# An order table that starts from the key weights, in a one-core adaLN mixer

## The chip, the cores and the metric

The kernel runs on one core of a Trainium2 chip. A core has a matrix engine (TensorE, PE, with a weight load queue PEld beside it), a vector engine (VectorE, DVE), a scalar engine (ScalarE, ACT), a general engine (GpSimd, POOL) and a sync engine (SyncE, SP) that issues transfers. Each engine works through its own list of instructions in order; engines wait for one another through semaphores. Data lie in on-chip memory of 128 partitions; matmul results go to eight banks of PSUM. The metric is device time of one launch in microseconds (us).

## The reference, cut to what matters

One sequence x of 2048 rows of 448, a conditioning row c, bfloat16 throughout:

```python
mod = (silu(c) @ w_mod).reshape(1, 6, 1, 448)      # sa, ca, ga, sb, cb, gb
h = layernorm(x) * (1 + ca) + sa
x = x + ga * A(h, wqkv, w_phi, wo)
h = layernorm(x) * (1 + cb) + sb
x = x + gb * B(h, w_in, w_sp, b_sp, w_out)

def A(h):            # 16 heads of 28
    q, k, v = h @ wqkv, by head
    phi(t) = [softmax(t @ w_phi), softmax(-t @ w_phi)]        # 56 features
    o = phi(q) @ (phi(k)^T v) / (phi(q) . sum(phi(k)) + 1e-6)
    return o @ wo

def B(h):
    z1, z2 = split(gelu(h @ w_in))                  # 896 each
    g = w_sp @ layernorm(z2) + b_sp                 # w_sp is 2048 x 2048, over the rows
    return (z1 * g) @ w_out
```

## The kernel before, in words

The rows are taken as 16 tiles of 128. The whole computation of the fast path is a set of small step functions (`fast_path`, from L538), and a written table, `ORDER` (L482), says in which order they are issued. A word of the table is step:arguments@PSUM bank/engine; the engine is V for DVE, S for ACT, G for POOL and Y for SP, and a step without one has a fixed engine. The loop at L1245 to L1257 walks the table once, under a manual schedule, so the instructions of each engine stand in the order in which the table names their steps, and an engine that waits for one step holds all later ones. Nothing else sets the order. The words, by stage:

- **Loads.** `ld:...` issues one transfer (L664 to L682). wq, wk, wv are the 448x448 parts of wqkv, x0 to x5 the rows of x in groups of 1, 1, 2, 4, 4 and 4 tiles, phi is w_phi, wsa, wca, wsb, wcb are the shift and scale parts of w_mod, wmga and wmgb its two gates, wo, win0, win1, wout the remaining weights, bsp the bias of the row mixing. `W:t,u` (L1076) loads a piece of w_sp with a transposing transfer. The transfers of SP and ACT use eight semaphores in turn.
- **Front.** `du:n` are n matmuls on zeros (L734). `ct` and `ce` make silu(c). Wq and Wk are multiplied by w_phi beforehand ("folded"): `FTq`, `FTk` transpose the raw weights on PE (L824), `ETq`, `ETk` copy the transposes out of PSUM (L828 or L830), `PFq`, `PFk` multiply by a block-diagonal w_phi (L840), `EPq`, `EPk` copy the folded blocks out (L828, L830). `csA`, `ccA` (L769) turn shift and scale into columns, `esA` and `ecA` copy them; `SHk`, `SHq`, `SHv` (L783) make the shift's row of each weight and `SCk`, `SCq`, `SCv` (L801, L803) scale its rows. `csB`, `ccB`, `esB`, `ecB`, `SHw`, `SCw` do the same for w_in, and `YB`, `YE` for its first half.
- **First layer norm.** `l1s` statistics on DVE, `l1e`, `l1r`, `l1a` the factors and the normalised rows; `X` and `XE` transpose tiles 0 to 3 on PE, `T1` the others by transposing transfers on SP.
- **Attention sums.** Per tile: `kM` (L881), `kE`, `kF` two exponentials on ACT (L884), `kS` their row sums on DVE (L895), `kR` reciprocals (L899), `kP` the products (L902, DVE or POOL), `vM` and `vC` (L889, L892), and `kA` (L912), which adds the tile to one accumulator in PSUM. After the last `kA`, `KV` copies the accumulator out (L918, L920). `gr:0`, `gr:1` (L940) and `ge` spread the two gates over the rows; `wos`, `wts` (L946) multiply them into wo and w_out.
- **Attention output.** `qM` (L929), `qE`, `qF` (L934) for the queries; per tile `nM` (L957), `nX`, `nC`, `nS`, `nV`, `nT` (L976, the product of numerator and reciprocal), `nA` (L982), a transposing transfer `T2` (L863), and `wM` or `wN` (L992; `wN` adds x by one more matmul, L990), `wR` (L997, L999), `wQ` sums of squares.
- **Second layer norm and w_in.** `lA` to `lD`, `l2r`, `l2a`, the transfer `T3`, then `zM` and `zG` (z2, L1038), `zQ`, `zA` to `zD`, `zW`, `zN` its layer norm, `yM` and `yG` (z1, L1068, L1071).
- **Row mixing and output.** `gM` (L1084) multiplies w_sp by the last column block directly; the first six column blocks go by seven products instead of eight for a 2x2 split: `tT`, `sS` form differences and sums of the operands, `pM` (L1148) the products, `pc`, `pb` (L1171, L1172, POOL), `uA`, `uB`, `uW`, `cA` (L1175, DVE) combine them and `cX` (L1200) multiplies by z1. `oM` (L1097) is the product with w_out, `oE` adds x, `oD` writes a tile of 112 KB out; the last tile is done in two halves by `oH`, `oG` (L1106) and `oF` (L1110).

`guard`, `guard2`, `guard3` and `read` decide whether the sums were in a safe range; a general path stands behind them and is not run on these inputs.

Of the kernel before, what the change touches and what calls it, by code (L numbers as in the profile page):

```python
# [1305 lines left out]
```

## Time and profile before

| | us |
|---|---|
| median of 3 runs | 250.22 (249.93 to 250.77) |
| the profiled execution's own time | 250.54 |
| its span | 248.7 |
| PE busy | 239.2 (96%) |
| DVE busy | 187.5 (75%) |
| ACT busy | 115.7 (47%) |
| POOL busy | 128.3 (52%) |
| chain that ended last | PE 81%, DVE 10%, ACT 4%, DMA 2% |

The span runs from the first instruction to the last; the execution's own time holds also what lies around it, 1.8 us here. A row of the timeline gives start, length, engine, line, operation, output and input, and in square brackets the idle time before it with what ended it. A row with "x12" joins twelve instructions that follow one another. The chain of waits follows the end of the span back from each step to what released it. Matmuls overlap at their ends, so the length of a group of them is somewhat more than the distance to the next.

### The profile page before, as it was taken

Reading aid. Unit: us, or ns where it says so; the run is one execution under the profiler, and the core shown is the slowest. Engines: PE = TensorE matmul, PEld = TensorE weight load, DVE = VectorE, ACT = ScalarE, POOL = GpSimd, SP = SyncE. Lnnn points to the kernel's source line nnn. Section 1 sums busy time; section 2 is a strip of 40 time slices with the busy share of each in tenths; the row PEclk is TensorE's granted clock in tenths of the full one; section 3 lists DMA queues with packets and bytes.
Section 4 is the critical chain, followed back from the end, with each engine's and each line's share of the span. In section 5 each row is a group of like instructions: output and inputs, shape, how many; then the busy total and the mean of one; then the engine's idle time right before and its main releaser. Section 6 shows DMA issues by size and latency. Waiting matters only on the chain.

```text
span 248.7 us, 4220 instructions
## 1 busy us (share of the span) xinstructions
PE 239.2 (96%) x1520; PEld 127.2 (51%) x1528; DVE 187.5 (75%) x374; ACT 115.7 (47%) x231; POOL 128.3 (52%) x172
## 2 busy tenths in 40 slices
PE   8899999999889999999999999999999999999992
PEld 6755566566535555544444444444444544444652
DVE  2889998977988988967357985858899754727652
ACT  3999887738889888787878110000010000000000
POOL 4768878576678556747855449601541901401000
PEclk9999999999999999999999999999999999999998
DMA  7998989970595634782100960009930120000022
GB/s 190 307 279 166 206 171 234 204 191 0 100 167 115 128 88 86 168 154 60 42 0 4 152 102 0 3 0 155 187 79 3 55 74 0 3 0 3 18 78 86
DMA packets 68800, 25.23 MB, mean 101 GB/s; under 512 B 58401, under 2 KB 68642, under 8 KB 68770
## 3 DMA queue, kind: packets, MB, share of 16 engines
q1 hardware_dynamic: 68160, 24.41, 48.9%
q10 hardware_dynamic: 610, 0.46, 0.6%
q8 instruction: 14, 0.23, 0.4%
q14 instruction: 16, 0.13, 0.2%
HBM read 8.87 MB, written 1.84 MB: 43 GB/s over the span
## 4 chain that ended last, share of the span: by engine, by line
PE 81%; DVE 10%; ACT 4%; DMA 2%; issue 1%; DVEq 0%; ACTq 0%; SPq 0%
PE f_psum L1148 29%; PE f_psum L1068 10%; PE f_psum L1038 9%; PE f_psum L1097 8%; PE f_psum L1084 6%; PE f_psum L992 4%; PE f_psum L929 3%; PE f_psum L881 3%; DVE f_ksum L895 2%; PE f_psum L889 2%; DVE f_t L976 2%; DMA f_oo<-f_oo 2%; PE f_psum L734 2%; DVE f_phik L902 1%; PE f_psum L957 1%; PE f_psum L783 1%
## 5 line engine op out<-in xcount | busy, mean ns | idle before, releaser
L1148 PEld LDWEIGHTS <-f_z2n 128*128 128x128 bf16 x192 | 18.7, 98 | 22.4
L1148 PE MATMUL f_psum<-f_wsp,f_z2n 128*128 128x512 bf16 x119 | 27.1, 379 | 0.1
L1068 PE MATMUL f_psum<-f_hT,f_win 112*128 112x512 bf16 x112 | 26.3, 379 | 0.0
L1038 PE MATMUL f_psum<-f_win,f_hT 112*128 112x448 bf16 (+1 forms) x128 | 26.1, 352 | 0.0
L1148 PE MATMUL f_psum<-f_hT,f_Eq 128*128 128x512 bf16 x92 | 22.3, 379 | 0.2
L1168 ACT COPY f_Eq<-f_psum 128x512 f32<-128x512 f32 x4 | 2.3, 586 | 40.0 <-PE f_psum L1148 40.0
L1097 PE MATMUL f_psum<-f_wout,f_z1T 128*128 128x448 bf16 x105 | 20.4, 352 | 0.0
L1071 ACT ACTIVATE f_z1T<-f_psum,f_yb 128x512 bf16<-128x512 f32 x28 | 17.8, 686 | 3.3 <-PE f_psum L1068 3.3
L934 ACT ACTIVATE f_Eq<-f_psum 112x1024 bf16<-112x1024 f32 x16 | 16.1, 1037 | 5.1 <-PE f_psum L929 5.1
L1038 PEld LDWEIGHTS <-f_hT 112*128 112x128 bf16 (+1 forms) x128 | 12.3, 97 | 11.7 <-DVE f_t L976 0.2
L1200 POOL TENSOR_TENSOR f_z1T<-f_gb,f_z1T 128x512 bf16<-128x512 f32 x6 | 7.8, 1310 | 19.3 <-DVE f_gb L1175 19.3
L976 DVE TENSOR_TENSOR f_t<-f_psum,f_w 128x896 bf16<-128x896 f32 x16 | 16.9, 1086 | 0.5
L895 DVE TENSOR_REDUCE f_ksum<-f_E 128x32 f32<-128x896 bf16 x16 | 16.8, 1066 | 0.6 <-ACT f_E L884 0.5
L1068 PEld LDWEIGHTS <-f_win 112*128 112x128 bf16 x112 | 10.9, 98 | 12.2
L884 ACT ACTIVATE f_E<-f_psum 128x448 bf16<-128x448 f32 x32 | 15.7, 565 | 2.6 <-PE f_psum L881 2.5
L1042 ACT ACTIVATE f_z2g<-f_psum 128x896 bf16<-128x896 f32 x16 | 14.6, 915 | 4.9 <-PE f_psum L1038 3.5
L929 PE MATMUL f_psum<-f_hT,f_Wq 113*128 113x512 bf16 (+1 forms) x64 | 15.2, 378 | 0.0
L1148 PEld LDWEIGHTS <-f_Eq 128*128 128x128 bf16 x96 | 9.4, 98 | 11.3
L992 PE MATMUL f_psum<-f_win,f_oo 112*128 112x448 bf16 x64 | 14.1, 352 | 1.1 <-DMA f_oo<-f_oo 0.9
L1097 PEld LDWEIGHTS <-f_z1T 128*128 128x128 bf16 x105 | 10.2, 98 | 9.4
L1113 DVE TENSOR_TENSOR f_xpad<-f_psum,f_x 128x448 bf16<-128x448 f32 x15 | 9.0, 618 | 7.5 <-PE f_psum L1097 7.5
L1175 DVE TENSOR_TENSOR f_z2g<-f_psum,f_z2g 128x512 f32<-128x512 f32 x12 | 8.3, 688 | 8.4 <-PE f_psum L1148 8.0
(214 smaller groups left out, 513.5 us busy)
## 6 DMA issues: line engine op xcount, KB each, us to landing
...
f_x<-in_A_x_dram SPq DMA_DIRECT2D x3, 448.0 KB, 8.3
f_wmg<-in_w_mod_dram SPq DMA_DIRECT2D x2, 392.0 KB, 7.2
...
f_wq_raw<-in_A_wqkv_dram ACTq DMA_DIRECT2D x1, 392.0 KB, 3.9
```

What stands on the lines that cost most here:

```text
L884: nc.scalar.activation(out=Er[i % NR][:, s, :], in_=ps["k" + str(i)][:, 0, 0:D], func=ACT.Exp, scale=1.0 - 2.0 * s)
L895: nc.vector.tensor_reduce(out=ksum[:, i], in_=Er[i % NR][:].rearrange("p s (c f h) -> p (s c) h f", c=4, h=HP), axis=AX.X, op=ALU.add)
L929: nc.tensor.matmul(t[:, u, :], lhsT=Wq[0:KR[m], m, cc * CB:cc * CB + P], rhs=hT[0:KR[m], 4 * st:4 * st + 4, m, :], start=(m == 0), stop=(m ...
L934: nc.scalar.activation(out=Eq[st // 2][0:CB, 2 * c2:2 * c2 + 2, s, (st % 2) * 512:(st % 2 + 1) * 512], in_=ps["q" + str(n)][0:CB, :, :], f ...
L976: nc.vector.tensor_tensor(out=tr[i % 2][:], in0=numv(i)[:, :, :, 0:DH], in1=wr[i // 2 % 2][:, i % 2].unsqueeze(3).to_broadcast([P, 2, H, D ...
L992: nc.tensor.matmul(t[:, 0, 0:D], lhsT=oT[0:CB, i % 4, cc, :], rhs=wo_s[0:CB, cc, :], start=(cc == 0 and not with_x), stop=(cc == KC - 1))
L1038: nc.tensor.matmul(t[:, hf, 0:D], lhsT=hT[0:KR[m], i, m, :], rhs=win_s[0:KR[m], m, FH + hf * D:FH + (hf + 1) * D], start=(m == 0), stop=(m ...
L1068: nc.tensor.matmul(t[:, 0, :], lhsT=win_s[0:CB, m, fc * P:(fc + 1) * P], rhs=hT[0:CB, 4 * st:4 * st + 4, m, :], start=(m == 0), stop=(m == ...
L1071: nc.scalar.activation(out=stage_b()["z1T"][:, fc, st * 512:(st + 1) * 512], in_=ps["y%d_%d" % (st, fc)][:, 0, :], func=ACT.Gelu_apprx_tan ...
L1084: nc.tensor.matmul(g[:, 0, 0:b - a], lhsT=later["z2n"][:, s_, fc * P:(fc + 1) * P], rhs=wspT[t][:, s_, a:b], start=(s_ == 0), stop=(s_ == ...
L1097: nc.tensor.matmul(ps["o" + str(t)][:, 0, 0:D], lhsT=later["z1T"][:, fc, t * P:(t + 1) * P], rhs=wout_s[:, fc, :], start=(fc == 0), stop=( ...
L1148: nc.tensor.matmul(t[:, 0, :], lhsT=b[:, j, f * P:(f + 1) * P], rhs=a[:, j, :], start=(PSTART[k] and j == 0), stop=(j == NH - 1), skip_gro ...
```

## The change

Only the table `ORDER` is changed; the steps and the work they do stay as they are, apart from the numbers below. It has been written anew from the front on:

- wk is the first transfer, on ACT's queue, and wq the third on SP; x0 comes before x1, and then phi, wq, x1, x2, wca, wsa, x3, wv, wmgb, x4, x5, wmga and the rest follow on SP.
- 18 matmuls on zeros instead of 33, 15 of them ahead of the first transposes. `FTk`, `PFk` stand ahead of `FTq`, `PFq`; `ETk:1`, `ETq:0` and `XE:0` go to DVE, `EPq:2` and `XE:2` to ACT.
- The first `kM` is that of tile 1; `gr:1` stands directly behind it (before: in the middle of the attention sums), `gr:0` later.
- `csB`, `ccB`, `YB` and `SHw:3` stand ahead of `KV`; before they stood behind it.
- `kP` is split 8 on DVE and 8 on POOL instead of 10 and 6. In all 105 steps go to another engine. Four tiles use `wN` (2, 4, 8, 9; before three: 0, 1, 2), so there is one such matmul more.
- `W:1,*` come later among the `T2` and `T3`, and `ld:bsp` earlier.
- From the first `gM` on PE's order is the same. `pb` on POOL goes 0,2, then 0,0, then 0,1, with one `cX` between the first two and two between the second (before: 0,0, 0,1, 0,2).
- The outputs `oD` of tiles 1, 2, 6, 8 and 14 and the first half of tile 15 go out on ACT's queue, the second half of tile 15 as the last on SP (before: all on SP but that second half).

The diff, cut to its core:

```diff
 ORDER = """
-ld:wq/S m3 m2b/G m1/V m2a/G du:18@0 du:3@5 ld:c/S ct@2 tbl ce:1 ce:2 m5 ld:x1/Y l1s:1 ce:3 l1e:1,2/V l1r:1,2 l1a:1/G FTq:1@5 ETq:1/S FTq:0@6 ETq:0/S
-du:6@3 ld:wk/Y FTk:0@3 ETk:0/S FTk:1@5 ETk:1/S ld:phi/Y bd/V PFq:0@6 EPq:0/S PFq:1@1 EPq:1/S ld:x2/Y ld:x0/Y l1s:0 l1s:2 ce:4 l1e:0,1/G l1r:0,1 du:6@7
-l1s:3 l1e:2,4/V l1a:0/G PFk:1@4 PFk:2@2 EPk:2/S PFk:0@3 EPk:0/S EPk:1/S PFq:2@0 PFk:3@2 l1r:2,4 l1a:3/G EPk:3/S PFq:3@7 X:0@6 EPq:3/S ld:x3/Y l1s:5
-l1s:7 X:1@5 ld:wsa/Y csA@3 esA EPq:2/V X:3@2 XE:3/S l1s:4 SHk@4 ld:wca/Y ccA@2 ecA SCk:3/V XE:0/S XE:1/S SCk:0/S SCk:1/S SCk:2/V l1s:6 SHq@1 SCq:1/V
-SCq:2/S SCq:3/S SCq:0/S scb l1a:2/G X:2@6 XE:2/V ld:wv/Y ld:x4/Y SHv@2 SCv:2/V SCv:3/V l1e:4,8/G l1r:4,8 l1a:4/G SCv:0/S l1a:6/G kM:0@4 kM:1@7 kF:1
-l1a:5/G SCv:1/S kE:1 kE:0 kF:0 kM:2@5 qM:0@A1 kE:2 qF:0 qE:0 ld:wmga/Y l1s:8 l1s:10 l1s:9 gr:0@0 ld:x5/Y ld:wo/Y kF:2 ge:0 vM:3@6 vM:1@4 vC:1 W:0,0
-l1a:7/G m4 T1:4,6 kS:1 ld:wmgb/Y l1s:11 kS:0 kR:1 l1e:8,12/G kR:0 l1s:13 kP:1/G l1r:8,12 l1a:11/G T1:6,8 vM:0@7 l1s:12 kP:0/V kS:2 kR:2 W:0,5
...
-ld:win0/Y wos:2/G kR:6 kP:5/V vM:7@4 vC:7 kS:7 kR:7 kP:7/V kM:8@6 kF:8 kE:8 kS:8 gr:1@7 W:0,4 kP:6/G kR:8 vM:6@5 kM:9@2 kE:9 kM:11@4 kF:9 kM:10@6 ge:1
...
-kA:13@A0 kR:14 kP:14/V kA:14@A0 wts:1/G kP:15/V kA:15@A0 KV:1 qM:3@C qE:3 KV:0 csB@3 esB ccB@4 ecB nM:0@A1 nX:0 qF:3 nC:0 YB@1 YE W:0,7 nM:1@A2
-wos:0/G wts:5/G wts:4/G SCw:1,0/G nX:1 nC:1 nS:0 nV:0 nT:0 nA:0/G T2:0,1 nT:1 nA:1/V T2:1,2 SCw:2,0/S SHw:2@0 SCw:0,2/S qM:4@C qF:4 nM:2@A0 nX:2
-SHw:3@3 SCw:0,3/V nC:2 SCw:3,1/G qE:4 nM:3@A2 nX:3 SCw:2,1/S SCw:1,1/S qM:5@A1 qE:5 nM:4@C W:1,1 nC:3 nS:1 nV:1 nT:3 nT:2 nM:5@A2 nX:5 wN:0@0 nC:5
-wN:1@1 nX:4 nC:4 nS:2 qF:5 wR:0/S wts:0/G wR:1/S nA:2/V nA:3/G T2:2,4 nV:2 nT:5 nA:5/G nT:4 W:1,3 nM:7@A1 nX:7 nC:7 wQ:0/S nM:6@A2 nX:6 qM:6@A0 wQ:1/S
-lA:0,2/G lB:0,2/G lC:0,2/G lD:0,2/G SCw:3,0/S qF:6 nA:4/V T2:4,6 nC:6 nS:3 nV:3 nT:6 W:1,7 qE:6 wM:3@6 wN:2@7 wR:2/S l2r:0,2 l2a:1/G T3:1,2 nT:7
-wR:3/V wQ:3/S qM:7@A2 qE:7 qF:7 nA:7/V l2a:0/G lA:2,4/G lB:2,4/G T3:0,1 wM:4@7 wQ:2/V lC:2,4/V lD:2,4/V l2r:2,4 l2a:2/G wR:4/V nA:6/V T2:6,8 l2a:3/G
...
-pM:0,1,1@5 sS:0,3,1/V pM:0,0,2@6 gG:1,6 sS:0,2,0/V pb:0,0 tT:3,2,4/V cA:0,0,11 cX:0,0,11/G sS:0,3,0/V pM:0,2,1@1 pc:0,1 pM:0,1,2@5 cA:0,1,11 pc:0,2
-pM:0,2,2@1 sS:0,4,0/V pM:0,0,6@0 uB:0,0 uA:0,0 tT:4,4,6/G pM:0,0,7@2 uW:0,0 pM:0,1,6@4 guard pM:0,0,4@2 cA:0,0,21 cX:0,1,11/G W:2,1 pb:0,1 pM:0,1,7@3
-pM:0,2,6@7 uB:0,1 uW:0,1 uA:0,1 wts:2/V pM:0,1,4@3 pM:0,2,7@6 W:3,4 W:3,6 W:2,0 W:3,2 pb:0,2 uA:0,2 uB:0,2 uW:0,2 W:3,0 wts:6/V pM:0,0,5@0 W:2,2
...
-oD:1/Y oD:4/Y oD:6/Y oD:2/Y cX:1,1,11/G pM:1,0,5@0 cA:1,0,22 cX:1,0,22/V pM:1,2,4@6 pM:1,1,5@4 cA:1,1,22 pM:1,0,3@0 cX:1,1,21/G oD:3/Y pM:1,2,5@7
...
-gG:2,6 gM:3,6@5 cA:1,2,21 cX:1,2,21/V oM:8,0,7@3 oE:8 oM:9,0,7@2 oE:9 gM:4,6@6 gG:3,6 gG:4,6 oD:8/Y oM:10,0,7@0 read oM:11,0,7@4 oE:11 oE:10
-oM:12,0,7@3 oE:12 oM:13,0,7@2 oE:13 oD:7/Y oD:10/Y oD:11/Y oD:9/Y oD:13/Y oD:12/Y oM:14,0,7@1 oE:14 oD:14/Y oH:15,0@5 oG:15,0 oF:15,0/Y oH:15,1@6
-oG:15,1 oF:15,1/S hint
+m4 du:6@0 du:3@2 du:3@5 ld:wk/S ld:x0/Y l1s:0 m5 m2a/G ld:c/S du:3@1 ld:phi/Y m1/V bd/V m2b/G l1e:0,1/G tbl FTk:1@7 ETk:1/V FTk:0@0 ETk:0/S du:3@5
+l1r:0,1 l1a:0/G ld:wq/Y FTq:1@1 ETq:1/S ld:x1/Y l1s:1 X:0@6 XE:0/V ld:x2/Y FTq:0@4 ETq:0/V PFk:3@2 EPk:3/S PFk:0@5 EPk:0/S PFk:2@0 ct@1 l1s:3
+l1e:1,2/G ce:1 PFk:1@3 ce:2 PFq:1@4 ce:3 EPk:2/S PFq:3@6 ld:wca/Y l1r:1,2 l1a:1/G EPk:1/S ce:4 scb m6 PFq:2@2 PFq:0@5 EPq:0/S X:1@0 EPq:2/S EPq:1/S
+EPq:3/S ld:wsa/Y csA@7 ld:x3/Y l1s:2 l1e:2,4/G l1r:2,4 l1a:3/G esA ccA@5 ecA XE:1/S l1s:5 SHk@3 SCk:2/S SCk:1/V SCk:0/S SCk:3/V m3 ld:wv/Y l1s:4 l1s:6
+l1a:2/G l1s:7 l1e:4,8/G l1r:4,8 l1a:6/G l1a:5/G l1a:4/G ld:wmgb/Y SHq@2 SCq:1/V SHv@7 SCv:1/V SCv:3/V SCv:0/S X:3@0 SCq:3/V XE:3/S SCq:2/S kM:1@6
+ld:x4/Y l1s:9 l1s:8 ld:x5/Y gr:1@4 kE:1 SCv:2/S l1s:11 l1s:10 l1a:7/G l1e:8,12/G l1r:8,12 X:2@7 XE:2/S ld:wmga/Y kM:3@5 kF:3 kE:3 W:0,5 kM:0@1 ld:wo/Y
+ge:1 SCq:0/S kE:0 kF:1 vM:1@3 kS:1 kR:1 kP:1/V l1a:9/G vC:1 kF:0 kS:0 kR:0 l1a:8/V vM:2@0 vC:2 l1a:10/G kP:0/G l1a:11/G kM:2@5 kE:2 kF:2 kS:2 vM:0@2
+l1s:12 kR:2 vC:0 l1s:13 gr:0@4 qM:1@C qE:1 qF:1 ge:0 wos:1/G kS:3 kR:3 wos:3/G qM:0@A1 qF:0 qE:0 kP:2/V T1:4,6 kM:4@5 vM:3@1 kE:4 vM:4@4 kM:5@6 kF:5
...
+qF:2 qE:2 ld:wcb/Y vM:5@6 vC:5 kM:7@4 kF:7 kE:7 csB@3 kA:3@A0 kS:4 wos:0/V wts:1/V kR:4 kP:4/V W:0,2 l1e:12,16/G l1r:12,16 l1a:13/G kS:5 l1a:15/G kS:6
+kR:5 kA:4@A0 kR:6 kM:9@6 esB vC:6 kP:5/V kE:9 kM:8@5 kP:6/V wts:2/V vM:7@7 kF:9 vC:7 kF:8 kS:7 T1:10,12 kM:10@4 ld:win0/Y kE:8 l1a:12/G kE:10 kF:10
+kA:5@A0 kR:7 wts:5/V kP:7/G T1:12,14 vM:10@2 kS:8 YB@5 l1a:14/G T1:14,16 kM:12@3 kM:11@7 kA:6@A0 vC:10 kA:7@A0 kE:11 kF:11 kS:9 kR:9 kP:9/G YE kR:8
+kS:10 ccB@6 kP:8/V ecB kF:12 wos:2/V kR:10 kM:13@2 vM:11@4 W:0,0 vM:9@5 kS:11 kR:11 vC:11 kE:12 kS:12 kE:13 ld:win1/Y vM:8@6 vC:8 kF:13 kS:13 vC:9
...
+SCw:3,0/S vC:13 vM:12@2 wts:0/G SHw:3@4 vC:12 vC:14 vM:15@5 kP:13/G kR:15 kA:12@A0 vC:15 kA:13@A0 kP:14/G kA:14@A0 SCw:0,3/V kP:15/V kA:15@A0 wts:4/V
+KV:1 SCw:1,0/G qM:3@A1 qE:3 KV:0 nM:0@A0 nX:0 nC:0 nM:1@A2 nX:1 qF:3 nC:1 nS:0 nV:0 nT:0 nA:0/G qM:4@C qE:4 qF:4 SHw:2@2 nT:1 nA:1/V T2:1,2 nM:2@A0
+nM:3@C SCw:0,2/S nX:2 nC:2 SCw:3,1/G nX:3 nC:3 nS:1 nV:1 nT:2 nA:2/G SCw:2,0/S T2:0,1 W:0,3 nT:3 nA:3/G ld:bsp/Y T2:2,4 SCw:2,1/S nM:5@A2 nX:5 qM:5@A1
+qE:5 nC:5 wM:1@1 wR:1/V wM:0@0 wR:0/V lA:0,2/G lB:0,2/G qF:5 nM:4@C nX:4 nC:4 nS:2 nV:2 nT:4 nA:4/G nT:5 nM:7@A1 nX:7 wQ:1/S wQ:0/S lC:0,2/G nC:7
+nA:5/V lD:0,2/G T2:4,6 l2r:0,2 l2a:0/G l2a:1/G qM:6@A0 qF:6 nM:6@C nX:6 nC:6 qM:7@A2 nS:3 qE:6 SCw:1,1/S qE:7 wN:2@1 wR:2/S T3:0,1 nV:3 nT:7 qF:7
+T3:1,2 nT:6 wM:3@2 nA:7/V wR:3/V nA:6/G T2:6,8 nM:9@A0 nM:8@C nX:8 nC:8 nX:9 nC:9 nS:4 nV:4 lA:2,4/G wQ:2/S nT:9 wQ:3/S lB:2,4/G nT:8 nA:8/V wN:4@3
+wR:4/S wQ:4/V wM:5@2 wR:5/V lC:2,4/G lD:2,4/G nA:9/G gt zM:0@A2 T2:8,10 zG:0 l2r:2,4 l2a:3/V l2a:2/G T3:2,4 zM:1@A0 zG:1 lA:4,6/G zA:0,2/G wM:7@7
...
+yG:3,3 sS:0,1,0/V sS:0,2,0/V pM:0,0,1@6 pc:0,0 pM:0,1,1@5 pc:0,1 W:2,5 sS:0,3,0/V pM:0,0,2@6 gG:0,6 gG:1,6 pM:0,2,1@1 pc:0,2 pb:0,2 sS:0,3,1/V
+pM:0,1,2@5 pM:0,2,2@1 pM:0,0,6@0 cA:0,0,11 cX:0,0,11/G cA:0,2,11 cA:0,1,11 pM:0,0,7@2 W:2,1 pb:0,0 cX:0,1,11/G cX:0,2,11/G pb:0,1 pM:0,1,6@4 uB:0,0
+uW:0,0 uA:0,0 uA:0,1 uB:0,1 pM:0,0,4@2 pM:0,1,7@3 uW:0,1 pM:0,2,6@7 uB:0,2 cA:0,0,21 pM:0,1,4@3 pM:0,2,7@6 W:3,4 sS:0,4,1/V uW:0,2 pM:0,0,5@0 W:3,6
+W:3,2 cA:0,1,21 cA:0,0,22 uA:0,2 cX:0,1,21/G wts:6/G pM:0,2,4@6 W:3,1 W:3,5 W:2,7 W:3,0 W:3,3 sS:0,4,0/V cA:0,2,21 pM:0,1,5@4 cA:0,1,22 cX:0,0,22/V
...
+cA:1,0,11 cX:1,0,11/G cX:0,0,21/G pb:1,0 pM:1,2,1@5 pc:1,2 pM:1,1,2@2 pM:1,2,2@5 oM:0,0,7@3 oE:0 oD:0/Y oM:1,0,7@6 oE:1 oD:1/S cA:1,2,11 cX:1,2,11/G
+oM:2,0,7@0 oE:2 oM:3,0,7@4 oE:3 pb:1,2 oM:4,0,7@3 oM:5,0,7@6 oD:2/S oE:5 oD:5/Y oM:6,0,7@0 oE:6 oM:7,0,7@4 sS:1,3,1/V cA:1,1,11 pM:1,0,6@0 uA:1,0
...
+cA:1,0,12 gM:2,6@1 cX:1,0,12/V gM:3,6@5 gG:2,6 gG:3,6 oM:8,0,7@3 oE:8 oD:8/S oM:9,0,7@2 oE:9 gM:4,6@6 gG:4,6 oM:10,0,7@0 oE:10 read oD:6/S oM:11,0,7@4
+oE:11 oD:9/Y oM:12,0,7@3 oE:12 oD:10/Y oM:13,0,7@2 oE:13 oD:13/Y oM:14,0,7@1 oE:14 oD:14/S oH:15,0@5 oG:15,0 oD:12/Y oF:15,0/S oD:11/Y oH:15,1@6
+oG:15,1 oF:15,1/Y hint
 """
```

55 lines of the change are left out of this document (24 added, 31 removed).

## The prediction

> **What bounds the kernel now.** I read the shares first, then the chain of waits, then the stretches, then PE's idle rows, then the first 20 us and the last 10 us of the timeline. The page, first two parts wanted:
>
> ```profile
> span 248.7 us, 4220 instructions
> ...
> PE 239.2 (96%) x1520; PEld 127.2 (51%) x1528; DVE 187.5 (75%) x374; ACT 115.7 (47%) x231; POOL 128.3 (52%) x172
> ```
>
> TensorE (PE) is the bound as a whole. Stretch by stretch (us from:to, length, then busy time of PE, PEld, DVE, ACT, POOL, granted PE clock, DMA share, GB/s):
>
> ```profile
> 30.00:40.00 10.00, 10.00 (x83) 6.05 (x82) 9.72 (x15) 8.71 (x18) 7.74 (x11) 1.00 0.91 162
> 60.00:70.00 10.00, 8.93 (x79) 5.47 (x78) 9.48 (x24) 8.89 (x21) 7.10 (x7) 1.00 0.53 72
> 90.00:136.00 46.00, 46.00 (x242) 22.66 (x240) 32.59 (x87) 38.31 (x81) 29.48 (x49) 1.00 0.40 81
> ```
>
> PE is full from 15 us on except around 60 to 80 us; from 20 to 53 us VectorE (DVE) is nearly full too. So time can be won in three places: before PE's first useful matmul, in the holes of 60 to 80 us, and after PE's last. The holes, from the timeline of PE (start, length, then the idle time before and its releaser):
>
> ```profile
> 64.74 0.59 PE L957 MATMUL f_psum<-f_KVbd,f_Eq 112*128 112x120 bf16 x8 [0.67 <-DVE f_t L976]
> 65.73 0.35 PE L990 MATMUL f_psum<-f_x,f_ident 128*128 128x448 bf16 x1 [0.40 <-DVE f_t L976]
> 71.38 0.93 PE L992 MATMUL f_psum<-f_win,f_oo 112*128 112x448 bf16 x4 [0.89 <-DMA f_oo<-f_oo]
> 80.58 1.67 PE L992 MATMUL f_psum<-f_win,f_oo 112*128 112x448 bf16 x8 [0.20 <-DVE f_t L976]
> ```
>
> They sum to 2.16 us. The front, from the timeline of all engines:
>
> ```profile
> 0.72 0.42 ACTq L655 DMA_DIRECT2D f_wq_raw<-in_A_wqkv_dram  x1
> 5.30 1.03 PE L824 MATMUL f_psum<-f_ident,f_wq_raw 112*112 112x112 bf16 x16
> 5.96 1.71 ACT L828 COPY f_wTq<-f_psum 112x896 bf16<-112x896 bf16 x2 [0.38 <-PE f_psum L824]
> 6.14 0.31 SPq L655 DMA_DIRECT2D f_wv<-in_A_wqkv_dram  x1
> 7.05 1.20 SPq L680 DMA_DIRECT2D f_wmg<-in_w_mod_dram  x1
> 9.15 1.00 ACT L828 CAST f_Wq<-f_psum 112x448 bf16<-112x448 f32 x2
> 10.00 1.89 ACT L828 CAST f_Wk<-f_psum 112x448 bf16<-112x448 f32 x4
> 14.80 0.92 PE L783 MATMUL f_psum<-f_wv,f_Ga 112*128 112x448 bf16 x4
> 15.55 2.45 PE L881 MATMUL f_psum<-f_Wk,f_hT 113*128 113x448 bf16 x12
> 19.10 1.09 DVE L895 TENSOR_REDUCE f_ksum<-f_E 128x32 f32<-128x896 bf16 x1
> ```
>
> The first k matmul (kM, L881) starts at 15.55. What it waits for is ScalarE (ACT): four copies of 0.86 each for the transposed weights (L828, the second pair from 7.56), then the folded blocks (L828), then the shift matmuls (L783). VectorE's chain of row sums (kS, L895) starts at 19.10. Landings, from the DMA view of the windows in which each was issued (KB, us to landing):
>
> ```profile
> f_wq_raw<-in_A_wqkv_dram ACTq DMA_DIRECT2D x1, 392.0 KB, 3.9
> f_wv<-in_A_wqkv_dram SPq DMA_DIRECT2D x1, 392.0 KB, 6.8
> f_wmg<-in_w_mod_dram SPq DMA_DIRECT2D x1, 392.0 KB, 10.6
> f_x<-in_A_x_dram SPq DMA_DIRECT2D x1, 448.0 KB
> ```
>
> So the first weight lands at 4.62, wv at 12.98 and the attention gate's weights (wmga) at 17.61.
>
> **The change part by part.** *Front.* Key weights now come first, on ACT's queue, at the place of the query weights: landing 4.6. The 15 dummy matmuls that now stand ahead of them end near 4.2, so they delay nothing. FTk runs 4.7 to 5.65 and its two copies go to ACT and DVE side by side (0.86 each) instead of four in a row on ACT: that takes 1.7 us out of ACT's list. The query weights go third on SP and land by about 6.3 (where wk, second there, landed: 1.17 + 5.0 = 6.1). ACT's nine fold copies and its exponential then run from about 7.9 to 12.0; they began at 9.15 before. Shifts for k and q follow at 11.6 and 12.0. SHv needs wv, and wv has the same bytes ahead of it as before, so it still lands at 12.98; before, SHv started at 14.80, so 1.8 us of slack were there, and they are used up. SHv at 13.0 takes 0.76, X:3 0.23: first kM at 14.05, 1.5 us earlier. What is late next is thus wv, and no reordering of folds can go below it.
>
> *gr:1 moved forward.* The matmul of the second gate is now second in PE's queue behind the first kM, and waits for wmgb, which now follows wv directly. Between wv's and wmga's landings 840 KB arrived (x4 and wmga) in 17.61 - 12.98 = 4.63 us; 392 KB take 2.16 at that rate: landing at 15.15, with PE there at 14.8: 0.35 us of stall. Behind it in PE's queue wait X:2 and all the other kM, and through them the row sums. From 0 (if it lands in time) to 2.8 (if it lands where the second transfer did, 17.6). A second stall of some 0.4, qM:0 behind a copy of v on ACT (vC:0), is my estimate from ACT's list. Together 0.75.
>
> *Work pulled ahead of the last kA.* The two column forms, YB and one SHw, which were PE's filler behind the attention sums, now run before:
>
> ```profile
> 55.33 0.94 PE L769 MATMUL f_psum<-f_scol,f_wm 112*128 112x1 bf16 x32
> 56.55 0.84 PE L794 MATMUL f_psum<-f_Gb,f_win 112*128 112x1 bf16 x28
> 57.66 0.92 PE L788 MATMUL f_psum<-f_win,f_Gb 112*128 112x448 bf16 x4
> ```
>
> and from the chain of waits, then from the DMA view of one window:
>
> ```profile
> 53.16 0.59 PE f_psum L912 x8
> ...
> 59.18 2.10 DVE f_t L976 x2
> ...
> 66.86 4.47 DMA f_oo<-f_oo
> ```
>
> ```profile
> f_oo<-f_oo SPq DMA_TRANSPOSE x2, 2.3
> ```
>
> Start to start the three are 0.78 (32 small matmuls less the overlap with the next), 0.70 and 0.76: 2.24 us. The first row of the chain is the last kA, ending at 53.6 on PE. In the new table it ends near 55.2 by two counts: PE's (14.05, plus 38.0 from the first kM to that end, plus 2.24, plus 0.75 of stalls) and DVE's (sums from 20.7, because kF:1 stands later, plus the old chain's 34.0, in which two products kP fewer and three gate scalings and three small copies more cancel about, plus the last kA). Both engines reach it together, so neither has slack.
>
> *From there to the first zM.* PE has 18.6 us of work there in the new table. What it waits for: the copy of the attention sums, qM:3 and nM:0, the normalisation on DVE (a pair of products takes 2.10), transposes by DMA, wM. My walk gives the first product's end 5.4 after the last kA, the first transpose at 6.9; with 2.3 to land (what the one at 62.70 took) it meets PE idle since 8.2: 1.1 us. Further waits for T2:0,1 and for T2:4,6, whose products stand behind the wR and nS of earlier pairs, bring it to 1.6 if ACT is never late, and to 3.05 if the exponentials' bank waits (two qE of about a microsecond between the wQ) fall where ACT's list puts them. A transpose behind a weight transfer took 4.47 and made 0.89 of the old holes; the new table moves four w_sp transfers later, which speaks for the low end. I take the middle, 2.4, against 2.16: +0.25.
>
> *Later.* Small waits at yM:0,6 (for wR:9) and nM:12 (for a PSUM bank read by yG:0,6) 0.4 by the walk; from zM:10 on I find none, and PE was full from 90 to 136 us. One wN more in place of a wM: +0.19. Engine moves of single steps (105) lie beside PE and cost nothing as long as it is the later one; if that cover goes, each costs its own 0.2 to 1 us.
>
> *Tail.* From the timeline of the last us:
>
> ```profile
> 240.00 5.02 SPq L1116 DMA_DIRECT2D out_dram<-f_xpad  x6
> 244.13 0.39 DVE L1106 TENSOR_TENSOR f_xpad<-f_psum,f_x 128x224 bf16<-128x224 f32 x1 [0.28 <-PE f_psum L1102]
> 244.55 0.38 ACTq L1110 DMA_DIRECT2D out_dram<-f_xpad  x1
> 245.12 0.71 SPq L1110 DMA_DIRECT2D out_dram<-f_xpad  x1
> ```
>
> SP issues six outputs one behind another until 245.02; the first half of the last tile, ready near 243.9, leaves only at 245.12, after the second half, and lands last. With five of the outputs on ACT both halves can leave by 244.55: -0.57 at best, 0 if SP, still with oD:13, 12 and 11 ahead of its half, is held as long again. I take -0.3.
>
> **Sum** for the profiled run (250.54, with a span of 248.7): -1.5 + 0.75 + 0.25 + 0.4 + 0.19 - 0.3 = -0.2. That run is 0.3 above the median of 250.22, so the median comes to about 250.0.
>
> **The rivals.** *(a) The front's gain is kept.* If wmgb is in time, the holes stay at their low end and the tail pays in full: -1.5 + 0.4 - 0.56 + 0.19 - 0.57 = -2.0, so 248.2. For it: the low ends are one mechanism, transposes landing at 2.3 as the later table leaves them alone; against it: both engines are full up to the last kA.
>
> *(b) wmgb comes late, and gr:1 blocks PE's queue.* Each us past 15.15 is a us for PE and DVE's sums. At 17.6 it adds 2.45: 252.5; it makes the kernel slower by over 0.3% from a landing near 16.1. For it: two transfers behind wv took until 17.61; against it: it is the first of them.
>
> *(c) GpSimd (POOL) is late in the last big stage.* The order there is now pb:0,2, one product with z1, pb:0,0, two more products, pb:0,1, and pM:0,1,4 on PE waits for the last through uW:0,1, by my walk with 0.35 us to spare. From POOL's timeline:
>
> ```profile
> 149.21 2.06 POOL L1200 TENSOR_TENSOR f_z1T<-f_gb,f_z1T 128x512 bf16<-128x512 f32 x1 [0.41 <-DVE f_gb L1175]
> 153.94 2.14 POOL L1171 TENSOR_TENSOR f_junk<-f_Eq,f_bsp 128x512 f32<-128x512 f32 x1
> 157.27 1.16 POOL L1171 TENSOR_TENSOR f_z2g<-f_oo,f_bsp 128x512 f32<-128x512 f32 x1
> ```
>
> The same addition takes 1.16 or 2.14, a product up to 2.06. Two such long ones in the row put PE 1.3 to 2.0 behind: 251.3 to 252.0, deciding from the point at which more than 0.35 + 0.95 is lost. Against it: uA and uB stand ahead and may use PE's slack elsewhere. [...]
>
> *(d) PE starts cold.* With 18 dummies for 33, the first useful matmuls could fall in a slow phase. In the trace 21 dummies took this long (row of the chain), while the clock column of the stretch reads 1.00:
>
> ```profile
> 1.23 3.85 PE f_psum L734 x21
> ```
>
> ```profile
> 1.23:4.00 2.77, 2.77 (x14) 1.97 (x15) 0.76 (x2) 1.49 (x2) 2.03 (x10) 1.00 0.78 216
> ```
>
> The first 14 take 2.77, 0.2 each, the other seven 1.08, 0.15 each at most, so the slow phase ends near 4.0, which 15 dummies still cover. If it lasted until all dummies were over and half the front's 3 us of shifts ran slow, +1.5: 251.5. [...]
>
> **How the numbers follow.** No change in this kernel is told from its spread within 0.3%, 0.75 us. Forecast 0.42 (249.3 to 250.8; faster 0.06, same 0.29, slower 0.07); (a) 0.30, faster; (b) 0.13, (c) 0.10, (d) 0.05, slower. Faster 0.36, same 0.29, slower 0.35. The range runs from (a), 248.2, to (c)'s upper end, 252.0; outside stay the better half of (a) and the worst of (b).
>
> **What would show it.** First kM at 14.05; gr:1's start against the landing of wmgb; the last kA near 55.2; holes before the first zM summing to 2.4; PE at gM:0 near 136.4 (136.31 before, in the chain); no idle row before pM:0,1,4; the last issue at 244.5 less whatever PE gained. Wrong would be: a first kM later than 14.6, holes over 4 us, or idle PE rows past 90 us.

## The result and the profile after

The changed kernel is slower: 254.33 us, median of 17 runs (251.84 to 256.58), against 251.05 (249.93 to 251.81) in 17 runs of the kernel before on the same chip. The ratio is 1.0105, with a 95% interval of 1.0082 to 1.0127; in two later comparisons, on two chips, it was 1.018, each against runs of before there. The 1.0105 goes by the 13 faster of the 17 runs, without four from 256.03 to 256.58; the two medians over all 17 give 1.013. The forecast of 250.0 was wrong, and its range ended at 252.0.

The first profile of the changed kernel is of the run of 256.19 us and has a stretch at a lower granted clock (40 to 50 us, below), so the readings are taken from a third profile of the same kernel, which has none. Its page, first two parts wanted:

```profile
span 251.1 us, 4195 instructions
...
PE 239.2 (95%) x1506; PEld 125.4 (50%) x1514; DVE 187.7 (75%) x374; ACT 115.1 (46%) x233; POOL 125.0 (50%) x170
```

Busy times are about those of before; the span is 2.4 us longer, so the loss within it is waiting. PE's timeline shows where (start, length, idle time before and its releaser; rows without idle time stand for milestones):

```profile
14.59 0.93 PE L881 MATMUL f_psum<-f_Wk,f_hT 113*128 113x448 bf16 x4
16.06 0.92 PE L940 MATMUL f_psum<-f_wmg,f_scb 112*128 112x448 bf16 x4 [0.55 <-DMA f_wmg<-in_w_mod_dram]
38.90 0.93 PE L881 MATMUL f_psum<-f_Wk,f_hT 113*128 113x448 bf16 x4 [0.32 <-DMA f_hT<-f_xpad]
41.74 0.85 PE L794 MATMUL f_psum<-f_Gb,f_win 112*128 112x1 bf16 x28 [0.73 <-DMA f_win<-in_B_w_in_dram]
56.73 1.17 PE L912 MATMUL f_psum<-f_vaug,f_phik 128*128 128x116 bf16 x16 [0.41 <-POOL f_phik L902]
64.41 1.00 PE L957 MATMUL f_psum<-f_KVbd,f_Eq 112*128 112x120 bf16 x16 [0.69 <-ACT f_Eq L934]
67.65 1.67 PE L992 MATMUL f_psum<-f_win,f_oo 112*128 112x448 bf16 x8 [0.50 <-DVE f_t L976]
72.31 0.59 PE L957 MATMUL f_psum<-f_KVbd,f_Eq 112*128 112x120 bf16 x8 [0.37 <-DVE f_t L976]
73.30 1.89 PE L929 MATMUL f_psum<-f_hT,f_Wq 113*128 113x512 bf16 x8 [0.40 <-DVE f_t L976]
```

The four holes from 64 us on answer to those of before. The four waits between the first kM (L881) and the last kA (the row at 56.73) are new, but for 0.13 us at the last kA before. In the milestones, us from the start of the span, they show as a last kA 4.1 us later:

| | before | after, first profile | second | third |
|---|---|---|---|---|
| first kM starts | 15.55 | 15.49 | 15.42 | 14.59 |
| first row sum kS starts | 19.10 | 21.34 | 21.32 | 20.84 |
| last kA ends | 53.75 | 60.60 | 58.46 | 57.89 |
| first gM starts | 136.15 | 141.08 | 139.28 | 138.44 |
| first half of the last tile, oH, starts | 242.59 | 247.53 | 245.73 | 244.89 |
| last output has landed | 247.21 | 252.42 | 250.81 | 249.62 |
| the execution's own time | 250.54 | 256.19 | 254.67 | 254.1 |

The difference between before and the third profile, 3.56 us, splits so: 2.29 up to the first gM (4.14 at the last kA, of which 1.85 come back by then), 0.01 from there to oH, 0.11 from oH to the last landing, and 1.15 behind the last landing.

### The profile page after: what moved, and what is told of

Its sections match the earlier page's. It is cut to its first block, busy times and chain, and to the rows that moved or that the text cites. A ratio compares the mean times of both kernels' runs of the same rounds, so it can differ in the third digit from the quotient of the medians.

```text
span 253.9 us, 4203 instructions
## 1 busy us (share of the span) xinstructions
PE 243.0 (96%) x1514; PEld 128.7 (51%) x1514; DVE 187.2 (74%) x374; ACT 114.9 (45%) x233; POOL 123.6 (49%) x170
## 3 DMA queue, kind: packets, MB, share of 16 engines
q10 hardware_dynamic: 1330, 1.03, 1.3%
HBM read 8.87 MB, written 1.84 MB: 42 GB/s over the span
## 4 chain that ended last, share of the span: by engine, by line
PE 81%; DVE 7%; DMA 4%; ACT 3%; POOL 1%; issue 1%; SPq 1%; DVEq 0%; POOLq 0%; ACTq 0%
PE f_psum L1148 29%; PE f_psum L1038 10%; PE f_psum L1068 10%; PE f_psum L1097 8%; PE f_psum L1084 5%; PE f_psum L992 5%; DMA f_win<-in_B_w_in_dram 2%; PE f_psum L929 2%; PE f_psum L957 2%; PE f_psum L881 2%; PE f_psum L889 2%; PE f_psum L912 2%; DVE f_ksum L895 2%; PE f_psum L824 1%; DVE f_phik L902 1%
## 5 line engine op out<-in xcount | busy, mean ns | idle before, releaser
L902 POOL TENSOR_TENSOR f_phik<-f_E,f_kr 128x896 bf16<-128x896 bf16 x8 | 13.5, 1688 | 10.6 <-ACT f_E L884 8.0
L1042 ACT ACTIVATE f_z2g<-f_psum 128x896 bf16<-128x896 f32 x16 | 14.6, 913 | 5.8 <-PE f_psum L1038 4.5
L881 PE MATMUL f_psum<-f_Wk,f_hT 113*128 113x448 bf16 (+1 forms) x64 | 14.7, 365 | 0.3 <-DMA f_hT<-f_xpad 0.3
L1200 POOL TENSOR_TENSOR f_z1T<-f_junk,f_z1T 128x512 bf16<-128x512 f32 x2 | 2.3, 1155 | 25.3 <-DVE f_junk L1175 25.3
```

The source lines that it names most:

```text
L881: nc.tensor.matmul(t[:, 0, 0:D], lhsT=hT[0:KR[m], i, m, :], rhs=Wk[0:KR[m], m, :], start=(m == 0), stop=(m == KC - 1))
L902: eng.tensor_tensor(out=pr[i % NR][:, 0:2 * D].rearrange("p (a f h) -> p a f h", a=8, h=HP), in0=Er[i % NR][:].rearrange("p s (c f h) -> p ...
```

## The experiments

Edits are given as moved words of the table. Ratios are to the kernel before on the same chip, with 95% intervals; they differ by up to 0.25% from the ratio of the medians. The runs below come from four chips, and the changed kernel ran again on two of them. On a third (`wts:3` moved, the late wout, the second front kernel) and a fourth (win0 early with the old outputs, the old table with two queues, the first front kernel, the first with the forms moved back) the only base is the kernel before.

**The same kernel again, twice.** No edit.

> The changed kernel once more, for a second trace. If the slow stretch after YB (the granted clock 0.83 between 40 and 50 us) is only a part of the loss, a run without it shows the first kM still near 15.5, the first kS near 21.3 and YB's wait of 1.6 for win0, at about 252 to 254 us. If that stretch is the whole loss, such a run is at about 250.

> The changed kernel again, as the base for wout_yb on the same chip: 1.01 to 1.02 of the kernel before, a wait of YB for win0 of 1.1 to 1.6.

Measured: 1.0182 (1.0132 to 1.0232) and 1.0182 (1.0146 to 1.0219). The times of the table above are these two. In the first profile PE waited longest for the w_in half, and the stretch behind that wait ran at a granted clock of 0.83; in the third it did not, with a wait of 0.73, below the 1.1 to 1.6 expected. The rows are PE's timeline and the stretch 40 to 50 us (busy time of PE, PEld, DVE, ACT, POOL, granted clock, DMA share, GB/s), of the first profile:

```profile
43.03 0.85 PE L794 MATMUL f_psum<-f_Gb,f_win 112*128 112x1 bf16 x28 [1.59 <-DMA f_win<-in_B_w_in_dram]
...
40.00:50.00 10.00, 8.41 (x93) 5.53 (x92) 7.83 (x15) 4.34 (x11) 5.02 (x4) 0.83 0.84 147
```

and the same stretch of the third:

```profile
40.00:50.00 10.00, 9.27 (x104) 5.66 (x102) 8.74 (x16) 5.69 (x14) 7.73 (x6) 1.00 0.79 164
```

From YB's start to the end of the last kA the first takes 17.57 us (60.60 - 43.03), the third 16.15 and the second, whose clock stays at 1.00, also 16.15: the stretch at the lower clock costs 1.4 us when it occurs. It adds to the loss, but the kernel is slower without it too.

**The first w_in half earlier.** YB (L794) needs win0, which is now issued behind wout, two pieces of w_sp and two transposes T1.

```diff
-... T1:8,10 W:0,4 qF:2 ... ld:wcb/Y vM:5 ... kP:4/V W:0,2 ... T1:10,12 kM:10 ld:win0/Y
+... T1:8,10 qF:2 ... ld:wcb/Y ld:win0/Y vM:5 ... kP:4/V ... T1:10,12 kM:10 W:0,4 W:0,2
```

> The load of win0 directly behind that of wcb on SP, with the two w_sp transfers W:0,4 and W:0,2 behind T1:10,12. Theory 1: YB's wait for win0 (1.59) and what follows it (slow matmuls, ACT and DVE idle behind kM:12 and kM:11) make most of the loss; then the wait goes, the clock stays at 1.00 from 40 to 50, the last kA ends some 3 us earlier and the time falls by 2 to 3.5, to about 251. Rival: DVE, whose row sums start 2.2 later than before, sets the last kA anyway; then the time falls by less than 1.

Measured: 1.0148 (1.0111 to 1.0186), beside 1.0182 of the same kernel without the edit on that chip. That is about 1 us of the time, as the rival had it, and the two intervals overlap. win0 lands at 37.74 and YB no longer waits, but the T1 behind it come later, and the next kM waits for one:

```profile
42.21 1.69 PE L881 MATMUL f_psum<-f_Wk,f_hT 113*128 113x448 bf16 x8 [0.64 <-DMA f_hT<-f_xpad]
```

The last kA ends at 57.59, against 57.89 in the third profile. So the wait for win0 is one of several for SP's transfers; taking one away brings out the next.

**More dummies in front.** `du:6@0` became `du:12@0`, 21 dummies ahead of the first transposes for 15.

> Six dummy matmuls more ahead of the first transposes (21 as before, 24 in all). Theory: PE's front runs cold (the sixteen transposes of wk take 1.74 against 1.03 for those of wq before); six more dummies end near 5.0, and the transposes go back to about 1.0, csA from 12.2 to 11 or so, the first kM to 14.9, as wv lands at 13.95; the time falls by 0.5. Rival: how long PE runs cold depends on the moment and not on the number of dummies; then the transposes stay at 1.7 and nothing changes.

Measured: 1.0268 (1.0218 to 1.0317), the worst of all. The front itself went as hoped, with the transposes at 1.03 and the first kM at 14.11:

```profile
1.24 4.66 PE L734 MATMUL f_psum<-f_zero 128*128 128x256 bf16 x21 [1.24 <-DVE f_zero L695]
5.69 1.03 PE L824 MATMUL f_psum<-f_ident,f_wk_raw 112*112 112x112 bf16 x16
...
41.75 0.85 PE L794 MATMUL f_psum<-f_Gb,f_win 112*128 112x1 bf16 x28 [1.49 <-DMA f_win<-in_B_w_in_dram]
```

The stretch of 40 to 50 us then had the clock at 0.83 again, and from YB to the end of the last kA it took 17.60 (59.35 - 41.75). At 116.81 PE waited 1.20 for a transpose. A first kM 1.4 us earlier than in the first profile bought nothing.

**Outputs.** Three kernels: the changed one with all outputs on SP in its own order (`oD` of 1, 2, 6, 8, 14 and `oF:15,0` from S to Y, `oF:15,1` to S); the kernel before with those outputs put on ACT, its order kept; and win0 early with order and queues of the outputs as before.

> The outputs back on SP, the second half of the last tile on ACT, as before the change. If the two queues of outputs won what I forecast, the time from the first oH to the end of the span grows by 0.3 to 0.6; if they won nothing, as the trace of after has it (from oH to the end 6.2 against 6.0 before), it stays within 0.2 or falls.

> The kernel before with nothing changed but the queues of the outputs: tiles 1, 2, 6, 8, 14 and the first half of 15 on ACT, the second half on SP. My forecast was -0.3. Rival, from the differences of time and span in the runs so far (1.8 to 1.9 with the outputs on SP, 2.2 to 3.0 with some on ACT): the span changes by less than 0.3 and the time grows by 0.5 to 1.0.

> win0 early as before in win0_early, and the last outputs in the order and on the queues of the kernel before. If outputs on ACT cost time outside the span, 254.2 falls by 0.6 to 1.0, to about 253.4, with a difference of time and span of 1.8 to 1.9; if not, it stays at 254.2.

Measured: 1.0233 (1.0161 to 1.0305), 1.0010 (0.9982 to 1.0038) and 1.0116 (1.0085 to 1.0148). On one queue the new order of outputs is bad: from oH to the last landing 6.3 us (247.70 to 254.00) for 4.73. On two queues it is about as good as the old order on one (4.62). SP's last issue starts 2.41 after oH (247.30 - 244.89), before 2.53 (245.12 - 242.59). ACT's and SP's timelines of the third profile:

```profile
246.19 1.00 ACTq L1110 DMA_DIRECT2D out_dram<-f_xpad  x1
247.30 0.39 SPq L1110 DMA_DIRECT2D out_dram<-f_xpad  x1
```

The kernel before with two queues has a span no shorter (median 248.95 against 249.0), but its median time lies 2.30 us above the span for 1.84. In the profiled executions, time less last landing is 3.3 us in five of the seven with all but the last half on SP (before: 250.54 - 247.21) and 3.9 in the other two, and 3.8 to 4.7 in all ten with outputs spread over both queues. So some 0.5 us behind the last landing goes with the second queue, though not with it alone. What happens there no trace shows.

**wout's place.** In the new table wout (784 KB) is issued at 26.4 us instead of 42.3, and its scaling with the gate (`wts`) follows among the attention sums. One kernel moves only POOL's first such scaling, `wts:3`, behind the normalisation of tile 15; the other moves `ld:wout` behind `ld:win1`, and with it six `wts`: five out of the attention sums (`wts:3` and `wts:2` to the row mixing, which the diff leaves out), and `wts:1` from DVE to POOL behind `kP:14`.

```diff
-qM:2 ld:wout/Y wts:3/G kA:0 ... wts:1/V ... wts:2/V ... wts:5/V ... ld:win1/Y vM:8 ... wts:0/G ... kA:15 wts:4/V KV:1
+qM:2 kA:0 ... ld:win1/Y ld:wout/Y vM:8 ... kP:14/G wts:1/G ... KV:1 SCw:1,0/G wts:5/G wts:4/G ... nA:2/G wts:0/G
```

> The changed kernel with one step moved: the gate scaling wts:3 on POOL, which waits for w_out (wout) to land, behind the factors and rows of the layer norm of tiles 12, 13 and 15. Theory 2: POOL's queue is what passes the late load on: wts:3 waits until 32, l1r behind it until 34.7, SP's transposes T1 behind that, win0's load behind those, YB behind win0. Then l1r comes 1.5 earlier, win0 lands 1 to 1.5 earlier and YB's wait is under 0.3; the time falls by 1 to 2.5 (slow clock included), to 253 to 254. Rival: the bytes of wout decide and not the queue; then win0 still lands near 42 and the time stays at 254 to 256.

> The changed kernel with w_out loaded behind win1 and its gate scalings back behind the attention sums (three of them off DVE's chain of row sums). Theory 2 with the bytes: win0 lands by 39, YB does not wait, the clock stays at 1.00, DVE's chain is 1.1 shorter, the last kA is near 56 (58.5 to 60.7 after) and the time 2 to 3 below that of after, at 252 to 253. Rival: the late start of the row sums and POOL's eight products hold the last kA at 57.5 or later; then less than 1 is won.

Measured: 1.0129 (1.0087 to 1.0170) and 1.0074 (1.0045 to 1.0103) on one chip. SP's timelines, of the third profile of the changed kernel with wout ahead of these rows, then of the late wout:

```profile
28.46 3.13 SPq L1076 DMA_TRANSPOSE f_wsp<-in_B_w_sp_dram  x1
36.20 0.58 SPq L655 DMA_DIRECT2D f_win<-in_B_w_in_dram  x1
```

```profile
27.80 1.31 SPq L1076 DMA_TRANSPOSE f_wsp<-in_B_w_sp_dram  x1
33.80 0.57 SPq L655 DMA_DIRECT2D f_win<-in_B_w_in_dram  x1
```

With wout under way, the issue of the next w_sp piece takes 3.13 us instead of 1.31 (3.45 to 3.79 in the first and second profile and with `wts:3` moved), and win0 leaves 2.4 us later. The chain of waits of the third profile had suggested another path: wout's landing, POOL's `wts:3`, POOL's normalisation behind it, SP's transpose, win0:

```profile
26.39 5.43 DMA f_wout<-in_B_w_out_dram
...
31.89 1.03 POOL f_wout L946
...
33.88 1.49 POOL f_rs L855
35.37 0.78 SPq L863
...
36.20 5.50 DMA f_win<-in_B_w_in_dram
41.69 0.05 issue
41.74 0.85 PE f_psum L794 x28
```

With `wts:3` out of the way POOL waits for DVE's statistics instead, as its timeline says, and win0 leaves no earlier (37.20, with a first kM at 15.61; 36.66 in the first profile, whose first kM is at 15.49):

```profile
33.22 0.23 POOL L851 TENSOR_SCALAR f_rs<-f_mv 128x4 f32<-128x4 f32 x1 [2.05 <-DVE f_mv L848]
```

So `wts:3` alone is not the cause. The early wout with what hangs on it makes 1.5 us of the late last kA; how much of that is SP's long issue and how much the scalings on DVE these two runs don't separate. At the first gM only 0.60 of the 1.51 is left (137.84 for 138.44), since the holes behind the last kA sum to 2.67 for 1.96; 1.69 to the kernel before stays. The ratio's interval overlaps the one that the changed kernel had in the result (1.0082 to 1.0127), so the gain is read from the traces. Without the early wout YB doesn't wait, PE has no idle row from 16.01 to 55.22, and the last kA ends at 56.38. PE's timeline of this kernel:

```profile
16.01 0.92 PE L940 MATMUL f_psum<-f_wmg,f_scb 112*128 112x448 bf16 x4 [0.67 <-DMA f_wmg<-in_w_mod_dram]
40.31 0.84 PE L794 MATMUL f_psum<-f_Gb,f_win 112*128 112x1 bf16 x28
55.22 1.17 PE L912 MATMUL f_psum<-f_vaug,f_phik 128*128 128x116 bf16 x16 [0.41 <-POOL f_phik L902]
```

**Column forms back behind the attention sums.** `YB`, `SHw:3` and their copies and scalings go back behind `KV`; in the second kernel `csB` and `ccB` too, on top of the late wout.

> YB and SHw:3 (with their copies and scalings) back behind KV, all else as after; csB and ccB stay ahead. Theory 1: what stands in PE's queue behind YB is what costs; then there is no wait for win0 and no slow clock, and the last kA comes at about 55.5 to 56.5 (1.46 of work less ahead of it than in win0_early, where it came at 57.6), with some of that work as filler behind it; time 253 to 254. Rival: DVE and POOL set the last kA (row sums from 20.7, eight products of 1.7 on POOL); then it stays at 57.5 or later although PE has less to do, and PE idles ahead of the kA.

> wout_late with csB, ccB, YB and SHw:3 (and their copies and scalings) back behind KV. Theory: the 2.24 of work pulled ahead of the last kA is lost as filler behind it, one for one; then the last kA comes 2.2 earlier than in wout_late (56.4), near 54.2, the holes behind it go, and the first gM stays within 0.5 of 137.8, the time at 1.005 to 1.009 of the kernel before. Rival: pulling it ahead costs in itself (both engines are full there) and putting it back wins 1 or more: 1.000 to 1.003.

Measured: 1.0248 (1.0169 to 1.0327) and 1.0122 (1.0092 to 1.0152); the second was expected at 1.005 to 1.009, and the changed kernel had 1.0182 on its chip. In the second the last kA ends at 55.29, 1.1 earlier than with the late wout alone, but the first gM starts at 137.90 against 137.84: what is taken from ahead of the last kA comes back behind it. It is no clean trade, since a kM there waits 1.26 for a transpose that the late wout alone hides. The first also shows that this is no cure for the waits; PE now stands before two kM:

```profile
40.45 0.93 PE L881 MATMUL f_psum<-f_Wk,f_hT 113*128 113x448 bf16 x4 [1.66 <-DMA f_hT<-f_xpad]
44.11 1.69 PE L881 MATMUL f_psum<-f_Wk,f_hT 113*128 113x448 bf16 x8 [1.55 <-DMA f_hT<-f_xpad]
```

**The front alone.** The new table up to the first kM, then the rest of the old table. The first try shared a PSUM bank between that kM and the transposes of tile 2 (`X:2@6`), so that tile 1's keys were formed of other values; the second has `X:2@5`. Two variants follow: x3 loaded right behind x2, and the copy of tile 2's transposes on ACT with the first exponentials ahead of `SCq:0`, three statistics of later tiles behind `kS:0`.

> The new front up to the first kM, and then the old table from there on. Theory: the front itself is the gain I forecast and the new order of the attention sums is the loss. Then the first kM is at about 14.4 (15.55 before), the last kA near 53 (53.75 before, 57.6 to 60.7 after) and the time 0.5 to 1 below that of the kernel before. Rival: ACT, which has still to scale the weights behind the first kM, keeps the first row sum kS at 19.1 or later; then the last kA does not move and the time is within 0.3 of before, or above it.

> front_only again, with X:2 in bank 5. (In front_only X:2 stood in bank 6 ahead of the exponentials of tile 1, so that they waited for it and tile 1's keys were formed of other values.) Theory: DVE's list decides. x3 lands 3.6 later in the new front, so the statistics of tiles 4 to 7 fall between 13 and 21 us and push the first row sum to 20.5 or later; then the last kA stays at 54 to 55 and the time within 0.3 of the kernel before, although the first kM comes 0.9 earlier. Rival: only the wait of the exponentials held it; then the first row sum is at 19.2 or earlier, the last kA at 53 and the time 0.8 below the kernel before.

> front_fixed with x3 loaded right behind x2, as early as before, ahead of wca and wsa. Theory: VectorE's statistics of tiles 4 to 7, which wait for x3, push the first row sum; then the first row sum moves from 20.6 to about 19.5 and the last kA from 54.5 to 53.5, unless csA, which now waits for wsa, takes 1 back from PE's front. Rival: the statistics fit in anyway; then the first row sum stays at 20.6 and the kernel is as fast as before or slower by what csA waits.

> front_fixed with the copy of tile 2 (XE:2) on ACT instead of VectorE, the first exponentials ahead of SCq:0 on ACT, and the statistics of tiles 8, 9 and 10 behind the first two row sums on VectorE. Theory: the 1.7 that PE waits for XE:2 goes and the first row sum starts at 18; but VectorE has the same work as before up to the last kA, so the last kA comes 0.5 to 1 earlier at most (53.6 to 54) and the time is 0.2 to 0.4% below the kernel before. Rival: it is the order alone; then the last kA comes at 53 and the time falls by 0.5% or more.

Measured: 0.9993 (0.9971 to 1.0016), 0.9990 (0.9968 to 1.0011), 1.0051 (1.0022 to 1.0080) and 1.0004 (0.9979 to 1.0030). In the second the first kM starts at 14.51, a microsecond before the old 15.55, and the gain is gone by the second group of kM, which waits for DVE's copy of tile 2's transposes. PE's timeline of the second kernel, then of the last:

```profile
18.13 0.93 PE L881 MATMUL f_psum<-f_Wk,f_hT 113*128 113x448 bf16 x4 [1.71 <-DVE f_hT L830]
```

```profile
18.63 0.93 PE L881 MATMUL f_psum<-f_Wk,f_hT 113*128 113x448 bf16 x4 [1.14 <-ACT f_hT L828]
```

In the second the row sums start 1.5 later than before, at 20.59, and the last kA ends at 54.52 (53.75). PE has no other idle row up to there, and its list alone gives that end: 14.51 + 38.20 of before + 1.71 + 0.23 for tile 2's transposes, which before stood ahead of the first kM, are 54.65. With x3 early the shift weights come 1.89 late, PE idles, and the granted clock drops in the two stretches behind (10 to 15 and 15 to 20 us):

```profile
12.44 1.01 PE L769 MATMUL f_psum<-f_scol,f_wm 112*128 112x1 bf16 x32 [1.89 <-DMA f_wm<-in_w_mod_dram]
...
10.00:15.00 5.00, 3.12 (x48) 2.05 (x46) 2.36 (x10) 2.98 (x7) 3.69 (x11) 0.74 1.13 271
15.00:20.00 5.00, 5.00 (x23) 2.45 (x21) 3.61 (x12) 2.83 (x6) 1.94 (x4) 0.58 1.11 275
```

In the last variant the transposes of wk took 1.75 and the first kM is at 15.58. The row sums start at 19.05, as before, and the last kA still ends at 55.02. PE is busy without a gap from 18.63 to there, and the same count (15.58 + 38.20 + 1.14 + 0.23 = 55.15) gives that end. So PE's wait for tile 2 sets it; that DVE's row sums do, as the theories of these runs had it, is not shown. No kernel tried beats the one before.

## Why the prediction was wrong

**The step that failed** is "Work pulled ahead of the last kA": it ends at 57.9 to 60.6 us, not 55.2. Both counts there added the moved matmuls and took it that their inputs would be there. The tail's term failed beside it (below). PE's count, from the first kM to the end of the last kA, was 38.0 + 2.24 + 0.75 = 41.0; the third profile has 43.3 (57.89 - 14.59). The kernel with the late wout gives the terms. Its 41.97 (56.38 - 14.41) is 3.77 more than before's 38.20: 2.24 for the three pulled matmuls, as priced; 0.67 wait of gr:1; 0.41 wait for kP:14 on POOL; and 0.23 for X:2, which stands behind the first kM in the new table and ahead of it in the old, and which I missed. That adds to 3.55, and 0.2 stays unplaced. With the early wout come 0.73 before YB and 0.32 before a kM in the third profile, 1.15 before YB in the second, 1.59 there and 1.4 of lower clock in the first. The prediction listed the loads as a part of the change and never asked when win0 lands, though YB and SHw cannot run without it: of a step moved forward, its transfers have to be moved forward too, and here another transfer was put ahead of them.

DVE's count failed beside it. The sums start at 20.84, as forecast (20.7), but take 37.05 to the end of the last kA for 34.65 before. DVE is busy for 34.59 of these 37.05 us, and was for 32.38 of 34.65. The prediction had three gate scalings and three small copies more cancel two products fewer. But the table has six gate scalings on DVE there for one, five of them ahead of the last product, and a scaling of w_in (0.58) besides. In the third profile two of the six take 1.15 and 0.82, while the others take 0.33 to 0.39. By DVE's timeline:

```profile
32.02 1.15 DVE L946 TENSOR_TENSOR f_win<-f_win,f_g_rep 112x448 bf16<-112x448 bf16 x1
37.93 0.82 DVE L946 TENSOR_TENSOR f_wout<-f_wout,f_g_rep 128x448 bf16<-128x448 bf16 x1
```

The six add up to 3.45 for 0.38. And the eight products left on DVE are hardly cheaper than the ten before: they add up to 7.08 in the third profile and 8.76 in the second, against 7.91. The longest of the second profile lies beside a product on POOL, by the two engines' timelines:

```profile
29.04 2.46 DVE L902 TENSOR_TENSOR f_phik<-f_E,f_kr 128x896 bf16<-128x896 bf16 x1
```

```profile
29.32 1.69 POOL L902 TENSOR_TENSOR f_phik<-f_E,f_kr 128x896 bf16<-128x896 bf16 x1
```

It ends at 31.50, 0.49 behind POOL's (31.01); the shortest DVE products take 0.60, and the longest of the kernel before takes 1.47. The prediction's count had no product of this length. Whether one of the two holds the other up here, and which engine would have ended later alone, the runs don't show.

**The front** was right in its mechanism and nearly in its size: first kM at 14.1 to 14.6 in seven of the eleven profiles with the whole change, against 14.05; wv, forecast at 12.98, landed there at 13.1 to 13.6. In the four others it is at 15.4 to 15.6: three had transposes of 1.74, and in the second profile wv landed at 14.40. But "1.5 us earlier" was passed through the sum as if the path led through the first kM. gr:1 starts at 15.7 to 16.5 in every profile with the whole change, whether the first kM is at 14.1 or 15.6: behind an early first kM it waits for wmgb, which lands between 15.1 and 16.5, and behind a late one it stands in PE's queue. The front alone, with gr:1 at its old place, is worth 0.999 of before; there PE waits for tile 2 instead. Nor does a shift ahead of the last kA pass whole to the first gM: the kernel before with two queues has its first kM 0.72 later than before (16.27), its last kA 0.42 later and its first gM 0.09 earlier (136.06), since one hole of PE behind the last kA is 0.27 there for 0.89. Rival (a) thus fell on the front itself.

**gr:1's wait** was forecast at 0.35 and measured 0.20 to 0.68, or none behind a late first kM. Rival (b) has the right mechanism and a mild price. **From the last kA on**, forecast and measurement agree: holes of 2.4 forecast, 1.96 measured (0.69 + 0.50 + 0.37 + 0.40), none of the 0.4 later, and from the last kA to the first gM 80.55 for 81.2. Shortening this part was the whole good of the pulled work; on top of the late wout, with the forms back behind `KV`, the first gM comes at the same time, so no net gain of it is seen.

**Rival (c)** did not occur: from the first gM to oH 106.45 us against 106.44, and no idle row. **Rival (d)** occurred in full (1.74 or 1.75) in four of the fourteen profiles with 15 dummies ahead of the transposes, and in part (1.16 to 1.52) in four more; in full, its price at the first kM is a microsecond, at gr:1 nearly nothing. The +1.5 for slow shifts was the author's estimate, and none of these four profiles shows it: in the first each of the three shifts takes 0.92, as before. With x3 early, behind the wait of 1.89, they take 1.68 to 1.70. PE's timeline, first profile, then third:

```profile
5.06 1.74 PE L824 MATMUL f_psum<-f_ident,f_wk_raw 112*112 112x112 bf16 x16 [0.45 <-POOL f_nm L852]
```

```profile
4.99 1.03 PE L824 MATMUL f_psum<-f_ident,f_wk_raw 112*112 112x112 bf16 x16 [0.44 <-DMA f_wk_raw<-in_A_wqkv_dram]
```

**The tail** was forecast at -0.3. Within the span it gained nothing (+0.1), and 1.15 was lost behind the last landing, of which the run of before with two queues shows 0.5; the rest is open. The prediction counted its first gM of 136.4 from 136.31 in the chain of waits, where PE's timeline has 136.15; by the timeline it is 136.24. So of the 3.8 us between 250.3, the forecast for a profiled run, and 254.1, 2.2 lie ahead of the first gM (138.44 for 136.24), 0.4 in the tail and 1.15 behind it.

What stays open: why the second queue costs time outside the span; what the remaining 0.6 us of the third profile's 5.1 between first kM and last kA are; what holds the first gM of the kernel with the late wout 1.69 behind that of before, beyond the waits counted above; and what makes the same kernel's ratio 1.0105 in the result (1.013 over all runs) and 1.018 in both later comparisons.
